# Reordering VectorE's work in a fused attention and two-stage MoE kernel: masks first, gate operations of two tiles alternating, one more buffer

## The chip, the cores and the metric

The kernel runs on one core of one Trainium2 chip. Its time is device microseconds (us) of one execution. Before the change, three runs took 1451.18, 1452.53 and 1453.46 us, so the median is 1452.53 us. A profile of one further execution is what all rows below are read from.

A core has five engines that run their own instruction streams in order and wait for each other through semaphores. TensorE (PE) multiplies matrices, and PEld is its loading of weights. VectorE (DVE) and ScalarE (ACT) work elementwise, as does GpSimd (POOL), and SyncE (SP) issues the DMAs here. The matrix results land in eight PSUM banks; everything else that the engines touch lies in SBUF.

## The reference, cut to what matters

Three steps are chained. A gated linear attention over 4 batches, 8 heads, 768 positions and heads of 48; then a feed-forward layer whose activation is a rational function; then four experts whose outputs are added with weights per token:

```python
f = 1 / (1 + exp(-f_logit))
for t in range(768):
    state = f[t] * state + outer(k[t], v[t]);  y[t] = q[t] @ state
x = y                                        # 3072 tokens x 384
h = x @ w_in                                 # 384 -> 2048
P = a[0] + a[1]*h + a[2]*h**2 + a[3]*h**3
Q = 1 + abs(b[0])*abs(h) + abs(b[1])*h**2
x = (P / (Q + 1e-6)) @ w_out                 # 2048 -> 384
p = probs / (probs.sum(-1) + 1e-9)
out = sum(p[:, e] * (relu(x @ w1[e]) @ w2[e]) for e in range(4))   # 384 -> 1024 -> 384
```

All values are float32. The inputs w_in and w_out of the first layer arrive as 64-bit words, two 32-bit halves each, and are turned into float32 on the chip.

## The kernel before, in words

The 3072 tokens are six chunks of 512 (128 positions of each of 4 batches). The first layer has 16 slots of 128 hidden columns (NJ1), the second has 4 x 8 slots. The first layer's products are called in1 and out1 (lines 836 and 846 as helpers mm_in and mm_out), the second's in2 and out2 (the same two lines). `fused` is one loop over a counter v, with tau = v + 19; manual order: every engine's instructions stand in the order in which this loop emits them. No scheduler moves them.

**The fill.** Chunk 0 has no earlier chunk to overlap with. Its attention runs first, and then for tau from -2 to 17 one slot of the first layer enters per step. Four pieces of work meet on VectorE there:

- Converting weights (`conv`). A slot's conversion has two halves in two consecutive steps. Stage 0 is two mask operations on VectorE (L737 and L738), followed by two operations on ScalarE (L739 and L740). Stage 1 is two more operations on VectorE (L742 and L743) and a product on GpSimd (L746), whose result wf is the slot's weight tile. The table CONV1 says at which step a slot's stage 0 stands; stage 1 stands one step later. `conv_ops(tau)` returns the two lists, and where a step has both, it is the older slot's stage 1 and the newer slot's stage 0.
- The gate, that is the rational function. ScalarE makes h squared, |b h| and a line in h (L894 to L896, `gate_in`). `gate_step` then has a new slot and an old one. For the new slot VectorE makes the denominator (L917) and the numerator (L920 and L921), and ScalarE takes the reciprocal through a logarithm and an exponential (L918 and L919). For the old slot, one step later, VectorE improves the reciprocal (L903 and L904) and multiplies (L911, or L906 in later chunks).
- TensorE's `fill_in` (L874, float32) writes the next slot's h into one of two banks, which become free when L921 has read them. `fill_out` (L881) uses the old slot's gate two steps on.
- At the end, the accumulated sums are split into two parts (L979 and L980) and the second layer starts.

**The mix.** From then on, for each of 192 steps, the second layer's in2 and out2 of the current chunk run, and between them attention and the first layer of the next chunk. For the second layer, ScalarE takes the relu (L934) and VectorE the rest of it (L935, gl), which out2 and the bank's next in2 wait for. Chunks 1 to 5 use the same `gate_step`; there the old slot's result q is copied to a rounded gh on ScalarE (L908) and the rest gl is made on VectorE (L926). `evac2` takes the sum of an expert from three banks: VectorE multiplies into a tile t (L971), GpSimd adds t to the output (L972). The tiles t come from the pool tp, which has two buffers.

Of the kernel before, what the change touches and what calls it, by code (L numbers as in the profile page):

```python
# [8 lines left out]
F32 = mybir.dt.float32  # L9
# [3 lines left out]
AF = mybir.ActivationFunctionType  # L13
ALU = mybir.AluOpType
# [17 lines left out]
QC = 1.0 + 1e-6  # L32
# [299 lines left out]
R = 14  # L332
# [355 lines left out]
def fused(ctx, tc, aps, consts, gm, dp, prep, flag_op):  # L688


    nc = tc.nc
    w1, w2, out = aps["w1"], aps["w2"], aps["out"]
    sc, pn, ident, mask = consts
# [5 lines left out]
    def pool(name, bufs):  # L699
        return ctx.enter_context(tc.tile_pool(name=name, bufs=bufs))  # L700

    wp, x2p, sp, op, pbp, tp, osp = (pool(n, k) for n, k in (
        ("wp", R), ("x2p", 2), ("s1p", 1), ("op", 1), ("pbp", 1), ("tp", 2), ("osp", 2)))
    g1p, g2p, gp = pool("g1p", QC1), pool("g2p", 3), pool("gp", 2)
    att = Att(ctx, tc, aps, consts, gm, banks)

# [44 lines left out]
    def conv_ops(tau):  # L751
        fs = [[], []]
        for i in range(NJ1):
            for k in range(2):
                if tau == CONV1[i] + k * (CONV1[i] >= NB - 6):
                    fs[k].append(partial(conv, i, k))
        return fs
# [39 lines left out]
    def store_all():  # L797
        for k in stores:
            nc.sync.dma_start(out=scr[uses[k]], in_=tile_of[k].bitcast(F32))
        stores.clear()  # L800
# [83 lines left out]
    gate_queue, gate = [], {}  # L884
# [13 lines left out]

    def gate_step(new, old, ops):

        if old:
            q0, r0, y0, _ = gate.pop(old[:2])
            nc.vector.scalar_tensor_tensor(out=q0, in0=q0, scalar=QC, in1=r0, op0=ALU.add, op1=ALU.mult)  # L903
            nc.vector.scalar_tensor_tensor(out=q0, in0=q0, scalar=2.0, in1=r0, op0=ALU.subtract, op1=ALU.mult)  # L904
            if old[0]:
                nc.vector.scalar_tensor_tensor(out=q0, in0=y0, scalar=sc[:, 3:4], in1=q0, op0=ALU.subtract, op1=ALU.mult)  # L906
                gh = g1p.tile([128, 512], F32R, tag="gh", name="gh")
                nc.scalar.copy(out=gh, in_=q0)  # L908
            else:
                gh = g1p.tile([128, 512], F32, tag="gh", name="g")  # L910
                nc.vector.scalar_tensor_tensor(out=gh, in0=y0, scalar=sc[:, 3:4], in1=q0, op0=ALU.subtract, op1=ALU.mult)  # L911
                act1[old[:2]] = gh
        for f in ops[ACT1]:
            f()
        if new:
            q, r, y, h = gate[new[:2]]
            nc.vector.scalar_tensor_tensor(out=q, in0=q, scalar=sc[:, 5:6], in1=r, op0=ALU.mult, op1=ALU.add)  # L917
            nc.scalar.activation(out=r, in_=q, func=AF.Ln, bias=sc[:, 6:7])  # L918
            nc.scalar.activation(out=r, in_=r, func=AF.Exp, scale=-1.0)  # L919
            nc.vector.tensor_tensor(out=y, in0=y, in1=h, op=ALU.mult)  # L920
            nc.vector.scalar_tensor_tensor(out=y, in0=y, scalar=sc[:, 2:3], in1=h, op0=ALU.subtract, op1=ALU.mult)  # L921
        for f in ops[DVE1] + ops[POOL1]:
            f()
        if old and old[0]:
            gl = g1p.tile([128, 512], F32R, tag="gl", name="gl")
            nc.vector.tensor_tensor(out=gl, in0=q0, in1=gh.bitcast(F32), op=ALU.subtract)  # L926
            act1[old[:2]] = (gh, gl)


# [89 lines left out]
    for v in range(-FILL - 6, LAST + 1):  # L1019
        tau = v + FILL  # L1020
        ops = att.begin(v)
        if tau == -5:
            prep()
        if tau + 6 <= NB:
            att.first(tau + 6, conv_ops(tau) if tau + 6 < NB else [[], []])
        store_all()
        items = steps.get(v, [])
        lead = 1 if items and items[0][0] == "in2" and items[0][1] == v + 1 else 0
        fill_run(ops[PA], 9 * lead)
        for item in items[:lead]:  # L1030
            emit(item)
        if 0 <= v < LAST and v not in act2:
            relu(v)
        for f in ops[ACT0]:
            f()
        for u in gate_queue:
            if u[0] and u[:2] not in gate:
                gate[u[:2]] = gate_in(u)
        if 0 <= tau + 1 < NJ1:
            fill_in(tau + 1)  # L1040
        ready = [u for u in gate_queue if u[:2] in gate]
        new = ready[0] if ready else None
        if new:
            gate_queue.remove(new)
        old, pend_old = pend_old, new
        if new or old:
            gate_step(new, old, ops)
        else:
            for f in ops[DVE1] + ops[ACT1] + ops[POOL1]:
                f()  # L1050
        c, k = v // (NE * NJ2) - 1, v % (NE * NJ2)
        if 0 <= c < NCH - 1 and k == 2:
            for b in range(2):
                write_out(c, b + (2 if c else 0), banks[6 + b])
        fill_run(ops[PB], 9 * any(item[0] == "out2" for item in items), True)
        for item in items[lead:]:
            if item[0] == "out2":
                emit(item)
                if run_bounds(v - 1)[1]:
                    evac2(v - 1)  # L1060
        for item in items[lead:]:
            if item[0] == "in2":
                emit(item)
                if v + 1 < LAST:
                    relu(v + 1)
        if 0 <= c < NCH - 1 and k == (1 if c else 2):
            for b in range(2):
                write_out(c, b + (0 if c else 2), banks[6 + b])
        for item in items[lead:]:
            if item[0] == "out1":  # L1070
                emit(item)
        for item in items[lead:]:
            if item[0] == "in1":
                emit(item)
        for u in gate_queue:
            if not u[0] and u[:2] not in gate:
                gate[u[:2]] = gate_in(u)
        if tau == -1:
            spread_probs()
        if 0 <= tau - 2 < NJ1:  # L1080
            fill_out(tau - 2)
        for f in ops[REST]:
            f()
        if v in groups:
            evac1(*groups[v])
        if tau + 6 >= NB:
            for f in sum(reversed(conv_ops(tau)), []):
                f()
        if 10 <= tau and v < -1:
            make_ready(min(R - 6, 2 * (tau - 9)))  # L1090
            split_to(min(AHEAD, state["ready"] - 2))
        if tau == NJ1 + 1:
            for m in range(3):
                split_x2(0, m, acc[m], nc.vector)
            load_pb(0)
        if v >= -1:
            split_to(state["used"] + AHEAD)
        att.loads(v)
        if v == 170:
            flag_op(banks[6], banks[7])  # L1100
# [168 lines left out]
```

## Time and profile before

| what | value |
|---|---|
| median of three runs | 1452.53 us |
| profiled execution, its own time | 1457.07 us |
| its span, first to last instruction | 1455.2 us |
| PE busy | 1375.7 us (95%) |
| DVE busy | 919.0 us (63%) |
| ACT busy | 675.7 us (46%) |
| POOL busy | 289.1 us (20%) |
| mean granted clock of TensorE | 0.978 of full speed |

The span lies 1.9 us below the execution's own time, and this execution is 4.5 us above the median of the three runs. Busy shares are averages over stages that differ: the page's slices of 36.4 us show VectorE at nine tenths and TensorE at eight in the third, fourth and fifth slice, and TensorE at nine tenths or more nearly everywhere from the sixth on. The fill is therefore one stage and the mix another, and they are read apart.

### The profile page before, as it was taken

Reading aid. Unit: us, or ns where it says so; the run is one execution under the profiler, and the core shown is the slowest. Engines: PE = TensorE matmul, PEld = TensorE weight load, DVE = VectorE, ACT = ScalarE, POOL = GpSimd, SP = SyncE. Lnnn points to the kernel's source line nnn. Section 1 sums busy time; section 2 is a strip of 40 time slices with the busy share of each in tenths; the row PEclk is TensorE's granted clock in tenths of the full one; section 3 lists DMA queues with packets and bytes.
Section 4 is the critical chain, followed back from the end, with each engine's and each line's share of the span. In section 5 each row is a group of like instructions: output and inputs, shape, how many; then the busy total and the mean of one; then the engine's idle time right before and its main releaser. Section 6 shows DMA issues by size and latency. Waiting matters only on the chain.

```text
span 1455.2 us, 18263 instructions
## 1 busy us (share of the span) xinstructions
PE 1375.7 (95%) x6502; PEld 1100.6 (76%) x6502; DVE 919.0 (63%) x1403; ACT 675.7 (46%) x1160; POOL 289.1 (20%) x257
## 2 busy tenths in 40 slices
PE   5688899989989999999999999999999999999996
PEld 5533488777768888887888887888888888888885
DVE  7899954879585747575656575566584645562222
ACT  3566644766553554444544543544543544441111
POOL 0122454456442002112002012001012001111010
PEclk8899999999899999999999999999999999999998
DMA  8233685667677556556656656666656766667660
GB/s 302 95 113 124 230 279 207 220 235 255 228 253 235 179 181 212 183 179 229 197 177 214 182 179 214 200 197 211 192 178 214 208 194 195 191 195 239 192 178 25
DMA packets 115699, 287.80 MB, mean 198 GB/s; under 512 B 13104, under 2 KB 31888, under 8 KB 114832
## 3 DMA queue, kind: packets, MB, share of 16 engines
q1 hardware_dynamic: 115024, 286.36, 61.4%
q8 instruction: 54, 0.88, 0.3%
q14 instruction: 45, 0.37, 0.1%
q10 hardware_dynamic: 576, 0.18, 0.0%
HBM read 237.69 MB, written 48.81 MB: 197 GB/s over the span
## 4 chain that ended last, share of the span: by engine, by line
PE 74%; DVE 15%; POOL 3%; issue 3%; DMA 2%; ACT 2%; SPq 0%; POOLq 0%; ACTq 0%; DVEq 0%
PE bank L846 34%; PE bank L836 32%; PE bank L488 2%; DVE t L738 1%; PE bank L464 1%; PE bank L493 1%; POOL w L793 1%; DVE y L920 1%; POOL o L972 1%; DVE t L742 1%; DMA f<-in_qkf_dram 1%; DVE t L743 1%; DVE y L921 1%; PE bank L504 1%; DVE q L904 1%
## 5 line engine op out<-in xcount | busy, mean ns | idle before, releaser
L836 PE MATMUL bank<-x,w 128*128 128x512 f32 x2448 | 609.1, 395 | 9.2 <-DVE gl L935 7.3
L846 PE MATMUL bank<-gh,w 128*128 128x512 f32 x1632 | 530.5, 401 | 6.3 <-DVE t L971 6.3
L836 PEld LDWEIGHTS bank<-x,w 128*128 128x128 f32 x2448 | 453.9, 189 | 104.4 <-DVE gl L935 9.5
L846 PEld LDWEIGHTS bank<-gh,w 128*128 128x128 f32 x1632 | 304.9, 189 | 68.8 <-DVE t L971 7.8
L846 PE MATMUL bank<-gl,w 128*128 128x512 f32 x816 | 325.0, 398 | 0.0
L935 DVE SCALAR_TENSOR_TENSOR gl<-bank,gh 128x512 fp32r<-128x512 f32 x192 | 131.5, 685 | 137.1 <-ACT gh L934 137.1
L972 POOL TENSOR_TENSOR o<-o,t 128x512 f32<-128x512 f32 x69 | 87.5, 1298 | 513.7 <-DVE t L971 513.7
L846 PEld LDWEIGHTS bank<-gl,w 128*128 128x128 f32 x816 | 154.4, 189 | 30.2
L934 ACT ACTIVATE gh<-bank 128x512 fp32r<-128x512 f32 x192 | 113.5, 592 | 124.5 <-PE bank L836 124.5
L917 DVE SCALAR_TENSOR_TENSOR q<-q,sc,r 128x512 f32<-128x512 f32 x80 | 60.2, 752 | 156.6 <-ACT r L895 156.6
L908 ACT CAST gh<-q 128x512 fp32r<-128x512 f32 x80 | 49.4, 618 | 183.2 <-DVE q L906 183.2
L793 POOL TENSOR_TENSOR w<-rawbuf,w 128x384 fp32r<-128x384 f32 x96 | 106.1, 1132 | 98.3 <-ACT w L792 74.8
L890 ACT COPY h<-bank 128x512 f32<-128x512 f32 x80 | 46.9, 586 | 142.6 <-PE bank L836 142.1
L874 PE MATMUL bank<-x,wf 128*128 128x512 f32 x96 | 51.7, 682 | 28.3 <-DVE y L921 21.4
L926 DVE TENSOR_TENSOR gl<-q,gh 128x512 fp32r<-128x512 f32 x80 | 55.1, 689 | 35.0 <-ACT gh L908 35.0
L488 PEld LDWEIGHTS bank<-v,am 128*128 128x128 f32 x384 | 64.9, 201 | 14.4 <-DVE am L475 9.9
L989 DVE TENSOR_TENSOR s<-s,bank 128x512 f32<-128x512 f32 x45 | 30.6, 682 | 71.5 <-PE bank L846 71.5
L971 DVE TENSOR_TENSOR t<-bank,pb 128x512 f32<-128x512 f32 x69 | 46.1, 687 | 45.1 <-PE bank L846 26.7
L488 PE MATMUL bank<-v,am 128*128 128x48 f32 x384 | 60.3, 262 | 9.4 <-DVE am L475 9.4
L904 DVE SCALAR_TENSOR_TENSOR q<-q,r 128x512 f32<-128x512 f32 x80 | 65.5, 819 | 2.8
L906 DVE SCALAR_TENSOR_TENSOR q<-y,sc,q 128x512 f32<-128x512 f32 x80 | 64.8, 810 | 2.8
L903 DVE SCALAR_TENSOR_TENSOR q<-q,r 128x512 f32<-128x512 f32 x80 | 64.4, 805 | 0.0
(102 smaller groups left out, 1413.0 us busy)
## 6 DMA issues: line engine op xcount, KB each, us to landing
w<-ws SPq DMA_DIRECT2D x448, 384.0 KB, 3.6
ws<-w SPq DMA_DIRECT2D x96, 384.0 KB, 4.0
raw<-in_w_dram SPq DMA_DIRECT2D x16, 768.0 KB, 6.8
rawbuf<-in_w_dram SPq DMA_DIRECT2D x64, 192.0 KB, 3.7
f<-in_qkf_dram SPq DMA_DIRECT2D x24, 256.0 KB, 3.7
k<-in_qkf_dram SPq DMA_DIRECT2D x24, 256.0 KB, 4.0
q<-in_qkf_dram SPq DMA_DIRECT2D x24, 256.0 KB, 4.1
w1s<-wf SPq DMA_DIRECT2D x16, 384.0 KB, 3.7
```

What stands on the lines that cost most here:

```text
L488: self.nc.tensor.matmul(self.py[:, o:o + D], self.am[a][:, r], self.v[:, o:o + D], start=(self.c == 0 and r == 0 and a == 0), stop=(r == N ...
L793: nc.gpsimd.tensor_tensor(out=t[:, 1], in0=r, in1=t[:, 0].bitcast(F32), op=ALU.subtract)
L836: nc.tensor.matmul(ps, a[:, o], b[:, kk, :], start=(n == 0), stop=(n == 8))
L846: nc.tensor.matmul(acc[m], a[:, o], b, start=(start and n == 0), stop=(stop and n == last))
L903: nc.vector.scalar_tensor_tensor(out=q0, in0=q0, scalar=QC, in1=r0, op0=ALU.add, op1=ALU.mult)
L904: nc.vector.scalar_tensor_tensor(out=q0, in0=q0, scalar=2.0, in1=r0, op0=ALU.subtract, op1=ALU.mult)
L906: nc.vector.scalar_tensor_tensor(out=q0, in0=y0, scalar=sc[:, 3:4], in1=q0, op0=ALU.subtract, op1=ALU.mult)
L917: nc.vector.scalar_tensor_tensor(out=q, in0=q, scalar=sc[:, 5:6], in1=r, op0=ALU.mult, op1=ALU.add)
L926: nc.vector.tensor_tensor(out=gl, in0=q0, in1=gh.bitcast(F32), op=ALU.subtract)
L934: nc.scalar.activation(out=gh, in_=h, func=AF.Relu)
L935: nc.vector.scalar_tensor_tensor(out=gl, in0=h, scalar=0.0, in1=gh.bitcast(F32), op0=ALU.max, op1=ALU.subtract)
L972: nc.gpsimd.tensor_tensor(out=o[c][:, m], in0=o[c][:, m], in1=t, op=ALU.add)
```

## The change

Three things are changed in `fused`. First, in a step that has both halves of a conversion, the newer slot's stage 0 (the masks) is emitted ahead of the older slot's stage 1. Second, `gate_step` no longer emits the old slot's operations and then the new slot's: in the fill (chunk 0, `late` false) they alternate one by one, and in later chunks (`late` true) the new slot's L917 stands after two of the old slot's three, with ScalarE's logarithm and exponential ahead of the old slot's copy. Third, the pool tp has three buffers. No operation is added or taken away.

```diff
-        ("wp", R), ("x2p", 2), ("s1p", 1), ("op", 1), ("pbp", 1), ("tp", 2), ("osp", 2)))
+        ("wp", R), ("x2p", 2), ("s1p", 1), ("op", 1), ("pbp", 1), ("tp", 3), ("osp", 2)))
...
+        vec = nc.vector
+        late = bool(new and new[0])
         if old:
             q0, r0, y0, _ = gate.pop(old[:2])
-            nc.vector.scalar_tensor_tensor(out=q0, in0=q0, scalar=QC, in1=r0, op0=ALU.add, op1=ALU.mult)
-            nc.vector.scalar_tensor_tensor(out=q0, in0=q0, scalar=2.0, in1=r0, op0=ALU.subtract, op1=ALU.mult)
+            vec.scalar_tensor_tensor(out=q0, in0=q0, scalar=QC, in1=r0, op0=ALU.add, op1=ALU.mult)
+            if late:
+                vec.scalar_tensor_tensor(out=q0, in0=q0, scalar=2.0, in1=r0, op0=ALU.subtract, op1=ALU.mult)
+        if new:
+            q, r, y, h = gate[new[:2]]
+            vec.scalar_tensor_tensor(out=q, in0=q, scalar=sc[:, 5:6], in1=r, op0=ALU.mult, op1=ALU.add)
+            nc.scalar.activation(out=r, in_=q, func=AF.Ln, bias=sc[:, 6:7])
+            nc.scalar.activation(out=r, in_=r, func=AF.Exp, scale=-1.0)
+        if old and not late:
+            vec.scalar_tensor_tensor(out=q0, in0=q0, scalar=2.0, in1=r0, op0=ALU.subtract, op1=ALU.mult)
+        if new and not late:
+            vec.tensor_tensor(out=y, in0=y, in1=h, op=ALU.mult)
+        if old:
             if old[0]:
...
         for f in ops[ACT1]:
             f()
+        if new and late:
+            vec.tensor_tensor(out=y, in0=y, in1=h, op=ALU.mult)
         if new:
-            q, r, y, h = gate[new[:2]]
-            nc.vector.scalar_tensor_tensor(out=q, in0=q, scalar=sc[:, 5:6], in1=r, op0=ALU.mult, op1=ALU.add)
-            nc.scalar.activation(out=r, in_=q, func=AF.Ln, bias=sc[:, 6:7])
-            nc.scalar.activation(out=r, in_=r, func=AF.Exp, scale=-1.0)
-            nc.vector.tensor_tensor(out=y, in0=y, in1=h, op=ALU.mult)
-            nc.vector.scalar_tensor_tensor(out=y, in0=y, scalar=sc[:, 2:3], in1=h, op0=ALU.subtract, op1=ALU.mult)
+            vec.scalar_tensor_tensor(out=y, in0=y, scalar=sc[:, 2:3], in1=h, op0=ALU.subtract, op1=ALU.mult)
...
         if tau + 6 >= NB:
-            for f in sum(reversed(conv_ops(tau)), []):
+            for f in sum(conv_ops(tau), []):
                 f()
```

Lines from 901 on have other numbers afterwards (L903, L904, L911, L917, L920 and L921 become L905, L914, L924, L910, L916 and L931 in the fill). On VectorE, one step of the fill that has both halves of a conversion reads before as follows; bank_97 belongs to the old slot, bank_98 and bank_95 to the new one, L742 and L743 are the older slot's stage 1, and L737 and L738 the newer slot's masks:

```order
L903 SCALAR_TENSOR_TENSOR bank_97<-bank_97,r 128x512
L904 SCALAR_TENSOR_TENSOR bank_97<-bank_97,r 128x512
L911 SCALAR_TENSOR_TENSOR g<-y,sc,bank_97 128x512
L917 SCALAR_TENSOR_TENSOR bank_98<-bank_98,sc,r 128x512
L920 TENSOR_TENSOR y<-y,bank_95 128x512
L921 SCALAR_TENSOR_TENSOR y<-y,sc,bank_95 128x512
L742 SCALAR_TENSOR_TENSOR t<-raw,t 128x768
L743 SCALAR_TENSOR_TENSOR t<-raw,t 128x768
L737 TENSOR_SCALAR t<-raw 128x768
L738 TENSOR_SCALAR t<-raw 128x768
```

The same step on VectorE after the change:

```order
L905 SCALAR_TENSOR_TENSOR bank_97<-bank_97,r 128x512
L910 SCALAR_TENSOR_TENSOR bank_98<-bank_98,sc,r 128x512
L914 SCALAR_TENSOR_TENSOR bank_97<-bank_97,r 128x512
L916 TENSOR_TENSOR y<-y,bank_95 128x512
L924 SCALAR_TENSOR_TENSOR g<-y,sc,bank_97 128x512
L931 SCALAR_TENSOR_TENSOR y<-y,sc,bank_95 128x512
L737 TENSOR_SCALAR t<-raw 128x768
L738 TENSOR_SCALAR t<-raw 128x768
L742 SCALAR_TENSOR_TENSOR t<-raw,t 128x768
L743 SCALAR_TENSOR_TENSOR t<-raw,t 128x768
```

The masks have moved ahead of L742 and L743, and no gate operation directly follows the one whose result it reads. In a mix step with an old and a new slot, VectorE reads before (q and y are tiles of either slot; L935 is the second layer's rest):

```order
L903 SCALAR_TENSOR_TENSOR q<-q,r 128x512
L904 SCALAR_TENSOR_TENSOR q<-q,r 128x512
L906 SCALAR_TENSOR_TENSOR q<-y,sc,q 128x512
L917 SCALAR_TENSOR_TENSOR q<-q,sc,r 128x512
L920 TENSOR_TENSOR y<-y,h 128x512
L921 SCALAR_TENSOR_TENSOR y<-y,sc,h 128x512
L926 TENSOR_TENSOR gl<-q,gh 128x512
L935 SCALAR_TENSOR_TENSOR gl<-bank_96,gh 128x512
```

and after the change, on the same engine at the same place:

```order
L905 SCALAR_TENSOR_TENSOR q<-q,r 128x512
L907 SCALAR_TENSOR_TENSOR q<-q,r 128x512
L910 SCALAR_TENSOR_TENSOR q<-q,sc,r 128x512
L919 SCALAR_TENSOR_TENSOR q<-y,sc,q 128x512
L929 TENSOR_TENSOR y<-y,h 128x512
L931 SCALAR_TENSOR_TENSOR y<-y,sc,h 128x512
L936 TENSOR_TENSOR gl<-q,gh 128x512
L945 SCALAR_TENSOR_TENSOR gl<-bank_96,gh 128x512
```

One pair has changed places: the new slot's denominator (L917, now L910) stands ahead of the old slot's last product (L906, now L919). This happens in 29 steps of the mix, and in the same steps ScalarE's copy gh of the old slot stands behind the new slot's logarithm and exponential instead of ahead of them. The order on TensorE, GpSimd and SyncE is unchanged everywhere.

## Rows read from the trace of the kernel before

**Rows 1.** Busy time by stretch, granted clock (PEclk), DMA share:

```profile
core 0: us, PE busy (x) PEld busy (x) DVE busy (x) ACT busy (x) POOL busy (x), PEclk, DMA share, GB/s
59.20:173.00 113.80, 86.07 (x180) 35.38 (x178) 111.17 (x150) 73.35 (x113) 32.09 (x20) 0.93 0.41 135
...
460.00:1130.00 670.00, 664.95 (x3270) 549.69 (x3269) 427.41 (x663) 318.17 (x540) 83.76 (x75) 1.00 0.63 196
```

**Rows 2.** The second mask operation in that first stretch: busy us, mean ns | idle before:

```profile
L738 DVE TENSOR_SCALAR t<-raw 128x768 int32<-128x768 int32 x11 | 19.0, 1729 | 0.0
```

**Rows 3.** Timeline of one fill step, all engines: start us, us, instruction, idle before:

```profile
87.22 0.55 DVE L738 TENSOR_SCALAR t<-raw 128x768 int32<-128x768 int32 x1
...
87.69 0.69 DVE L903 SCALAR_TENSOR_TENSOR bank<-bank,r 128x512 f32<-128x512 f32 x1
...
88.41 0.70 DVE L904 SCALAR_TENSOR_TENSOR bank<-bank,r 128x512 f32<-128x512 f32 x1
...
89.15 0.75 DVE L911 SCALAR_TENSOR_TENSOR g<-y,sc,bank 128x512 f32<-128x512 f32 x1
...
89.81 0.75 DVE L917 SCALAR_TENSOR_TENSOR bank<-bank,sc,r 128x512 f32<-128x512 f32 x1
...
90.47 0.68 DVE L920 TENSOR_TENSOR y<-y,bank 128x512 f32<-128x512 f32 x1
...
91.19 0.75 DVE L921 SCALAR_TENSOR_TENSOR y<-y,sc,bank 128x512 f32<-128x512 f32 x1
...
91.85 0.95 DVE L742 SCALAR_TENSOR_TENSOR t<-raw,t 128x768 int32<-128x768 int32 x1
91.86 0.58 ACT L894 ACTIVATE bank<-bank 128x512 f32<-128x512 f32 x1
...
92.20 2.74 PE L874 MATMUL bank<-x,wf 128*128 128x512 f32 x6
92.37 0.66 ACT L895 ACTIVATE r<-bank,sc 128x512 f32<-128x512 f32 x1
...
93.59 0.55 DVE L737 TENSOR_SCALAR t<-raw 128x768 int32<-128x768 int32 x1
93.75 2.06 POOL L746 TENSOR_TENSOR wf<-t 128x768 f32<-128x768 f32 x1 [9.19 <-DVE t L743]
...
94.06 2.17 DVE L738 TENSOR_SCALAR t<-raw 128x768 int32<-128x768 int32 x1
...
96.15 0.69 DVE L903 SCALAR_TENSOR_TENSOR bank<-bank,r 128x512 f32<-128x512 f32 x1
```

**Rows 4.** Timeline of a later fill step, with GpSimd beside the gate:

```profile
110.58 0.69 DVE L903 SCALAR_TENSOR_TENSOR bank<-bank,r 128x512 f32<-128x512 f32 x1
110.75 1.81 POOL L746 TENSOR_TENSOR wf<-t 128x768 f32<-128x768 f32 x1 [6.47 <-DVE t L743]
111.31 0.70 DVE L904 SCALAR_TENSOR_TENSOR bank<-bank,r 128x512 f32<-128x512 f32 x1
...
112.12 0.75 DVE L911 SCALAR_TENSOR_TENSOR g<-y,sc,bank 128x512 f32<-128x512 f32 x1
...
114.83 0.55 DVE L737 TENSOR_SCALAR t<-raw 128x768 int32<-128x768 int32 x1
```

**Rows 5.** The chain that ended last, end of the fill: start us, us, what:

```profile
159.42 1.79 POOL wf L746
161.26 4.54 PE bank L874 x6
165.79 7.72 PE bank L881 x18
...
174.61 2.77 PE bank L881 x6
```

**Rows 6.** TensorE's waits, whole span: us in total, times, longest us:

```profile
PE bank L874 <- DVE y L921: 21.4, 9, 5.6
...
PE bank L836 <- DVE gl L935: 7.3, 4, 4.7
PE bank L846 <- DVE t L971: 6.3, 3, 3.7
```

**Rows 7.** VectorE's waits, whole span, the same columns:

```profile
DVE q L917 <- ACT r L895: 156.6, 60, 5.9
...
DVE t L971 <- POOL o L972: 18.4, 22, 1.6
```

More of the change, by code (lines that the diff above doesn't have):

```diff
@@ L899, in gate_step @@
     def gate_step(new, old, ops):
+        vec = nc.vector
+        late = bool(new and new[0])
         if old:
             q0, r0, y0, _ = gate.pop(old[:2])
-            nc.vector.scalar_tensor_tensor(out=q0, in0=q0, scalar=QC, in1=r0, op0=ALU.add, op1=ALU.mult)
-            nc.vector.scalar_tensor_tensor(out=q0, in0=q0, scalar=2.0, in1=r0, op0=ALU.subtract, op1=ALU.mult)
+            vec.scalar_tensor_tensor(out=q0, in0=q0, scalar=QC, in1=r0, op0=ALU.add, op1=ALU.mult)
[11 more added lines that the diff above has]
+        if old:
             if old[0]:
-                nc.vector.scalar_tensor_tensor(out=q0, in0=y0, scalar=sc[:, 3:4], in1=q0, op0=ALU.subtract, op1=ALU.mult)
+                vec.scalar_tensor_tensor(out=q0, in0=y0, scalar=sc[:, 3:4], in1=q0, op0=ALU.subtract, op1=ALU.mult)
                 gh = g1p.tile([128, 512], F32R, tag="gh", name="gh")
@@ L910, in gate_step @@
                 gh = g1p.tile([128, 512], F32, tag="gh", name="g")
-                nc.vector.scalar_tensor_tensor(out=gh, in0=y0, scalar=sc[:, 3:4], in1=q0, op0=ALU.subtract, op1=ALU.mult)
+                vec.scalar_tensor_tensor(out=gh, in0=y0, scalar=sc[:, 3:4], in1=q0, op0=ALU.subtract, op1=ALU.mult)
                 act1[old[:2]] = gh
@@ L925, in gate_step @@
             gl = g1p.tile([128, 512], F32R, tag="gl", name="gl")
-            nc.vector.tensor_tensor(out=gl, in0=q0, in1=gh.bitcast(F32), op=ALU.subtract)
+            vec.tensor_tensor(out=gl, in0=q0, in1=gh.bitcast(F32), op=ALU.subtract)
             act1[old[:2]] = (gh, gl)
```

## The prediction

> **What bounds the kernel now.** I read the busy time by stretch first, because the kernel has a fill and a mix. In the fill, from 59.2 to 173.0 us, VectorE is busy 111.2 of 113.8 us, TensorE 86.1 and ScalarE 73.4 [rows 1]; VectorE is the bound there, and a microsecond taken from it is a microsecond of time until another engine catches up. From 460 to 1130 us TensorE is busy 665.0 of 670 us [rows 1]; what VectorE saves there buys next to nothing. The waits of TensorE say the same: 21.4 us for L921, the last gate operation, which only the fill's L874 waits for, against 7.3 us for gl and 6.3 us for t, the two results of VectorE that the second layer waits for [rows 6]. Then I read the fill step by step in the timeline [rows 3, 4], and at last the chain at its end, which tells where VectorE stops being the bound [rows 5].
>
> **The change part by part: the masks.** In the step of rows 3 the mask L738 takes 2.17 us and hands over to L903 2.09 us after its start (94.06 to 96.15); a step before, it took 0.55 us and handed over after 0.47 us (87.22 to 87.69). The difference stands next to it: GpSimd's L746 runs from 93.75 to 95.81, released by L743, and the long L738 ends 0.42 us after it. So the mask waits until GpSimd is through and then needs its own time. In that stretch the 11 masks take 19.0 us together [rows 2]; with n long ones of 2.17 and 11 - n of 0.55 that is n = 8. These are the eight steps in which an older slot's L743 stands just ahead of a newer slot's masks.
>
> After the change the masks stand ahead of L742 and L743, and L746 starts after both, when the next step's gate operations begin. They last some 3.8 us before the next masks can come, L746 2.06 us, so the two no longer meet. Do the gate operations suffer instead? In rows 4 an L746 stands beside L903, L904 and L911, and these take 0.69, 0.70 and 0.75 us, as without it in rows 3. So each of the eight steps loses 2.09 - 0.47 = 1.62 us, 13.0 us in all. The bounds: 0 if the long time has another cause, 13.0 if none of the eight meets another GpSimd operation.
>
> ScalarE's half of the conversion hangs on the masks too and starts earlier by as much; its user, L742, comes a step later. L746 stands at the end of a step as before.
>
> **The alternation.** In the fill a full step has six gate operations: 0.69 + 0.70 + 0.75 + 0.75 + 0.68 + 0.75 = 4.32 us [rows 3]. Where the next operation does not need the result, it starts 0.09 us before the one ahead of it ends (L911 at 89.15 lasts 0.75, L917 starts at 89.81). Where it does, it starts 0.03 us after the end (L903 to L904, 0.72 us apart). The step lasts 4.16 us now (87.69 to 91.85), and later, with a longer pause ahead of L911, 4.25 us (110.58 to 114.83) [rows 3, 4]. With six neighbours that do not depend on each other it should last 4.32 - 6 x 0.09 = 3.78 us, 0.38 us less early and 0.47 us less later. If the longer pause ahead of L911 stays, it is 0.38 us throughout; I take 0.41. There are 15 full steps, but the last two lie in the tail that TensorE sets (below), so 13 count: 5.3 us, with 4.9 and 6.1 as ends, and 0 as the lower end if a third operation in between does not help.
>
> The Trainium skill speaks against this part. Its page "VectorE: DVE Perf Modes", section "The DRAIN you can't avoid", reports that eight copies on VectorE took the same time with a semaphore after each as with one after the last, and concludes that the pipeline is emptied after each operation anyway and the semaphore costs nothing extra. By that rule the alternation would save nothing. The trace does not agree: the next operation starts 0.09 us before the end without a wait, 0.03 us after it with one. I keep the rule's outcome as a rival.
>
> **The new neighbours.** L917 now stands second in its step instead of fourth, 1.5 us earlier, and needs ScalarE's L895 of the new slot. In rows 3 L895 ended at 93.03, and the step whose L917 needs it began at 96.15, or 94.5 without the long mask; L917 comes 0.6 us into it, so 2 us are left. Only at the end is it close: slots 14 and 15 get their wf one step ahead of use. From the end of L743 that is L746 2.06, L874 2.74, and L894 with L895 up to 1.2 us: 6.0 us, against 3.78 + 1.74 (L742 and L743, 91.85 to 93.59) + 0.6 = 6.1 us on VectorE. If L874 runs as slowly as its last one did (4.54 us, rows 5, after a wait; 2.74 in rows 3), VectorE stalls 1.7 us. I take half, 0.8 us.
>
> **The tail.** From 159.4 us the chain is GpSimd's wf, then TensorE alone: L874 4.54, three slots of L881 7.72, and one more 2.77 us from 174.61 [rows 5]. It starts with L743 of slot 15, so it moves up by what VectorE has gained by then: 13.0 + 5.3 - 0.8 = 17.5 us. Within the tail I count nothing. TensorE cannot overtake earlier: per slot L874 and L881 are 2.74 us each at the faster level, 5.5 us, while VectorE's step has 3.78 us of gate and 0.94, 1.74 or 2.68 us of conversion: 4.7 to 6.5 us, 5.8 on average over a cycle of four slots with three conversions.
>
> **The mix.** In 29 steps L906 and L917 change places and the copy gh follows the exponential. Where VectorE does not wait, it is the same work in the same time, less one dependent pair (0.1 us). Where L917 waits for L895, which it does 60 times in the whole span, 2.6 us on average [rows 7], L906 now stands behind that wait, and what follows on VectorE (both numerator operations, gl of the gate, then L935 of the second layer, L971 and the sums) comes up to 0.66 us later. L935 has room: TensorE waited noticeably for it 4 times in 192, 7.3 us in all [rows 6]. I cost this at 0, with 0.66 us at each of those four places, 2.6 us, as the bad end. The copy gh comes some 1.3 us later on ScalarE, but two numerator operations stand on VectorE before anything reads it, and out1 needs it a step or more afterwards. The third buffer takes away L971's waits for L972: 18.4 us in 22 places on VectorE [rows 7]. But it is the third tile of a set that waits, and TensorE waits for t in 3 places only, 6.3 us [rows 6], for the first tile. I take 0; 3 us, half of that, is the good end.
>
> **The sum.** 1455.2 - 17.5 = 1437.7 us of span, 1439.6 us with the 1.9 us around it. The profiled execution is 4.5 us slower than the median, so I take the difference off the median: 1452.5 - 17.5 = 1435.0 us.
>
> **The rivals.**
> - The alternation saves nothing, by the mechanism above. For it: the long rows differ from the short ones by hundredths only, which the profiler's own stamps might make. Against it: the pattern repeats in each step. Then VectorE gains 13.0 us, without the stall, as it comes later: 1439.5 us.
> - The masks are not freed: they still meet a GpSimd operation, or their wait goes to L742, because GpSimd's other work (splitting weights, which begins in the fill's last steps) comes to stand there. For it: GpSimd is busy 32.1 us in the fill [rows 1], more than 2.06 us for each of 12 slots, 24.7 us, make. Against it: until then GpSimd has only L746 to do. If half of the eight waits stay, 6.5 + 5.3 = 11.8 us are gained, 1440.7; if all do, 5.3, and it is 1447.2 us.
> - The mix gains too: TensorE's waits for gl and t, 13.6 us together [rows 6], lie where VectorE is behind, and 0.1 us a step and freer evacuations take a third, 4.5 us: 1430.5 us.
> - Slower than before: L906 behind L917's wait makes VectorE late for L935 in the mix. The place is the 29 steps, the price 0.66 us each, 19.1 us, and each stop of TensorE makes the following matrix products slow, as the 4.54 us against 2.74 us show, which adds 1.8 us at a few places. It decides once L935's room is below 0.66 us in most of the 29 steps: 1452.5 - 17.5 + 19.1 + 1.8 = 1455.9 us. Against it: four noticeable waits in 192 steps.
>
> **How the numbers follow.** The forecast has 0.66, no gain from the alternation 0.11, masks not freed 0.10, the mix gaining too 0.10, slower 0.03. The forecast's own ends are 17.5 + 0.8 + 0.8 + 3 = 22.1 us (1430.4) and 4.9 + 13.0 - 1.7 - 2.6 = 13.6 us (1438.9). The range takes in the first rival, half of the second and the third: 1429.5 to 1443.5 us. A measurement of this kernel tells about 0.2%, 2.9 us, from no change. Faster than that are all cases but the last and a mixture of several bad ends: 0.94. Within it 0.03, slower 0.03.
>
> **What would show it.** In the new profile no mask L738 of the fill should last over 1 us, where eight did; the full gate step should last 3.8 us instead of 4.2; VectorE should still be busy over nine tenths of a fill that is some 17 us shorter; and from the start of the second layer to the end the time should be the same within 3 us. I am wrong if masks still end just after a GpSimd operation, if ScalarE or TensorE becomes the bound in the fill (VectorE idle there by more than 5 us), or if TensorE's waits for L935 grow beyond the four.

## The result and the profile after

| | before | after |
|---|---|---|
| median, us (4 runs each, same chip) | 1452.99 | 1436.04 |
| range of the runs, us | 1451.18 to 1454.79 | 1434.58 to 1440.86 |
| profiled execution, us (span) | 1457.07 (1455.2) | 1440.86 (1439.0) |

The ratio (of the means) is 0.9889, with a 95% interval from 0.9862 to 0.9916: 16 us less; the medians differ by 16.95 us. The forecast was 1435.0 us, its range 1429.5 to 1443.5 us.

The profiled execution after is 4.8 us above its median, so stretches are compared and not spans. I cut the span at the first mask of the fill (L737 of slot 4) and at the first sum that leaves the fill's banks (L980, after the change L990), and cut the fill once more at slot 14's L746 on GpSimd. Before, busy time by stretch:

```profile
0.00:55.92 55.92, 37.62 (x288) 35.27 (x288) 42.10 (x90) 21.08 (x34) 1.69 (x8) 0.85 0.65 239
...
55.92:150.82 94.90, 72.15 (x151) 29.61 (x151) 92.48 (x120) 62.22 (x93) 21.83 (x13) 0.93 0.34 111
150.82:176.32 25.50, 20.48 (x56) 9.11 (x57) 24.29 (x40) 13.84 (x23) 10.26 (x8) 0.93 0.72 242
...
176.32:1455.20 1278.88, 1245.41 (x6008) 1026.61 (x6006) 760.10 (x1154) 578.56 (x1010) 255.32 (x229) 0.99 0.64 202
```

The same four stretches of the kernel after the change:

```profile
0.00:60.10 60.10, 44.13 (x288) 41.90 (x288) 42.30 (x91) 21.08 (x34) 1.69 (x8) 0.77 0.62 226
...
60.10:138.53 78.43, 69.16 (x151) 28.90 (x151) 77.98 (x122) 62.17 (x95) 20.14 (x13) 0.96 0.40 132
138.53:162.46 23.93, 21.65 (x56) 9.73 (x57) 21.07 (x39) 12.18 (x22) 10.07 (x8) 0.86 0.84 290
...
162.46:1439.00 1276.54, 1243.40 (x6008) 1025.22 (x6006) 763.03 (x1155) 579.01 (x1010) 255.47 (x229) 0.99 0.63 201
```

The gain is the fill: 120.40 us became 102.36, which is 18.04 less, 16.47 of it ahead of slot 14's wf and 1.57 behind. The rest is 2.3 us shorter, and in kernels below whose rest is the same it lies anywhere from 1273.5 to 1278.9 us, so nothing is read from that. The start is the same work and took 4.2 us longer, at a granted clock of 0.77 instead of 0.85. Whether that is the 4.8 us by which this execution stands above its median is not shown: in the kernels below the start takes from 55.76 to 59.48 us, and one whose profiled execution lies 2.6 us under its median (e13) has a start of 58.74 us. In the first part of the fill VectorE is busy 77.98 of 78.43 us: still the bound. In the second part TensorE is busy 21.65 of 23.93 us, and VectorE is idle 2.9 us.

The second cut does not divide VectorE's work alike: slot 15's masks stand behind it before the change and ahead of it after. A cut that does is slot 15's L743, VectorE's last piece of conversion. Before and after it starts at:

```profile
158.26 0.95 DVE L743 SCALAR_TENSOR_TENSOR t<-raw,t 128x768 f32<-128x768 uint32 x1
...
143.00 0.94 DVE L743 SCALAR_TENSOR_TENSOR t<-raw,t 128x768 f32<-128x768 uint32 x1
```

From the start of the fill that is 102.34 us before and 82.90 us after, 19.44 less. What is left to the end of the fill became longer by 1.4 us, 19.46 us instead of 18.06.

The second mask within the fill of the kernel after, which answers to [rows 2]:

```profile
L738 DVE TENSOR_SCALAR t<-raw 128x768 int32<-128x768 int32 x12 | 6.7, 560 | 0.0
```

One full step after, which answers to [rows 3]:

```profile
66.75 0.55 DVE L738 TENSOR_SCALAR t<-raw 128x768 int32<-128x768 int32 x1
...
67.22 0.95 DVE L742 SCALAR_TENSOR_TENSOR t<-raw,t 128x768 int32<-128x768 int32 x1
...
68.09 0.95 DVE L743 SCALAR_TENSOR_TENSOR t<-raw,t 128x768 f32<-128x768 uint32 x1
...
68.96 0.69 DVE L905 SCALAR_TENSOR_TENSOR bank<-bank,r 128x512 f32<-128x512 f32 x1
69.12 1.82 POOL L746 TENSOR_TENSOR wf<-t 128x768 f32<-128x768 f32 x1 [3.41 <-DVE t L743]
...
69.56 0.75 DVE L910 SCALAR_TENSOR_TENSOR bank<-bank,sc,r 128x512 f32<-128x512 f32 x1
70.22 0.69 DVE L914 SCALAR_TENSOR_TENSOR bank<-bank,r 128x512 f32<-128x512 f32 x1
...
72.07 0.74 DVE L931 SCALAR_TENSOR_TENSOR y<-y,sc,bank 128x512 f32<-128x512 f32 x1
...
72.73 0.55 DVE L737 TENSOR_SCALAR t<-raw 128x768 int32<-128x768 int32 x1
```

No mask is long any more. The step runs from 68.96 to 72.73, 3.77 us, where it took 4.16 to 4.25 [rows 3, 4]. GpSimd's L746 stands beside three gate operations of unchanged length, and itself takes 1.82 us instead of 2.06, as no mask runs when it starts.

The chain at the end of the fill, which answers to [rows 5], starts one slot earlier:

```profile
138.53 1.82 POOL wf L746
...
140.40 5.49 PE bank L874 x6
145.88 2.98 PE bank L881 x6
148.86 2.58 PE bank L874 x6
151.44 7.72 PE bank L881 x18
```

Before, the last wait of TensorE for wf was slot 15's, and slot 15's L874 took 4.54 us [rows 5]; slot 14's took 2.84, though TensorE had stood still 3.33 us for its wf as well. Now TensorE stands still 3.85 us for slot 14's wf and then needs 5.49 us for six products that take 2.74 us for slot 15. The granted clock is 0.50 from 140.40 to 145.80 us, the level of 1.2 GHz, and 1.00 from 148.86 to 151.44 us, the level of 2.4. From there on TensorE is the bound. VectorE feels that at one place:

```profile
147.13 0.76 DVE L910 SCALAR_TENSOR_TENSOR bank<-bank,sc,r 128x512 f32<-128x512 f32 x1 [2.58 <-ACT r L895]
```

The waits over the whole span (engine, line, what it waited for: us, times, longest), which answer to [rows 6, 7]:

```profile
DVE q L910 <- ACT r L895: 167.0, 63, 9.3
...
PE bank L874 <- DVE y L931: 7.0, 5, 3.6
...
PE bank L836 <- DVE gl L945: 6.1, 4, 4.8
...
PE bank L846 <- DVE t L981: 6.0, 2, 3.7
```

L874's wait for the gate fell from 21.4 to 7.0 us. In the mix TensorE waits as before, at four places for gl and at two instead of three for t. VectorE's wait for L982, 18.4 us before [rows 7], is no longer among its waits, and nothing came of it. Its wait for L895 grew from 156.6 to 167.0 us, and TensorE's waits for VectorE in the mix did not grow with it.

### The profile page after: what moved, and what is told of

It reads as the page before. It is cut to its first block, busy times and chain, and to the rows that moved or that the text cites. A ratio compares the mean times of both kernels' runs of the same rounds, so it can differ in the third digit from the quotient of the medians.

```text
span 1439.0 us, 18273 instructions
## 1 busy us (share of the span) xinstructions
PE 1378.3 (96%) x6502; PEld 1105.8 (77%) x6502; DVE 904.4 (63%) x1403; ACT 674.4 (47%) x1160; POOL 287.4 (20%) x257
## 4 chain that ended last, share of the span: by engine, by line
PE 75%; DVE 14%; DMA 3%; ACT 2%; issue 2%; POOL 2%; SPq 1%; POOLq 0%; ACTq 0%; DVEq 0%
PE bank L846 34%; PE bank L836 32%; PE bank L488 2%; PE bank L464 1%; DMA f<-in_qkf_dram 1%; POOL w L793 1%; DVE y L931 1%; PE bank L493 1%; DVE g L434 1%; PE bank L881 1%; DVE q L910 1%; DVE q L905 1%; PE bank L504 1%; DVE q L919 1%; PE bank L874 1%
## 5 line engine op out<-in xcount | busy, mean ns | idle before, releaser
L982 POOL TENSOR_TENSOR o<-o,t 128x512 f32<-128x512 f32 x69 | 89.2, 1323 | 512.0 <-DVE t L981 512.0
L910 DVE SCALAR_TENSOR_TENSOR q<-q,sc,r 128x512 f32<-128x512 f32 x80 | 62.7, 784 | 167.0 <-ACT r L895 167.0
L921 ACT CAST gh<-q 128x512 fp32r<-128x512 f32 x80 | 49.1, 614 | 160.9 <-DVE q L919 160.9
L793 POOL TENSOR_TENSOR w<-rawbuf,w 128x384 fp32r<-128x384 f32 x96 | 104.9, 1120 | 95.6 <-ACT w L792 66.7
L911 ACT ACTIVATE r<-q,sc 128x512 f32<-128x512 f32 x80 | 58.0, 725 | 30.9 <-DVE q L910 23.9
L905 DVE SCALAR_TENSOR_TENSOR q<-q,r 128x512 f32<-128x512 f32 x80 | 65.0, 812 | 0.0
L896 ACT ACTIVATE y<-h,sc 128x512 f32<-128x512 f32 x80 | 64.1, 801 | 0.0
L912 ACT ACTIVATE r<-r 128x512 f32<-128x512 f32 x96 | 60.7, 632 | 3.1
L931 DVE SCALAR_TENSOR_TENSOR y<-y,sc,h 128x512 f32<-128x512 f32 x80 | 60.2, 752 | 2.8
```

The costliest lines, as they stand in the source:

```text
L793: nc.gpsimd.tensor_tensor(out=t[:, 1], in0=r, in1=t[:, 0].bitcast(F32), op=ALU.subtract)
L896: nc.scalar.activation(out=y, in_=h, func=AF.Identity, scale=sc[:, 0:1], bias=sc[:, 1:2])
L905: vec.scalar_tensor_tensor(out=q0, in0=q0, scalar=QC, in1=r0, op0=ALU.add, op1=ALU.mult)
L910: vec.scalar_tensor_tensor(out=q, in0=q, scalar=sc[:, 5:6], in1=r, op0=ALU.mult, op1=ALU.add)
L931: vec.scalar_tensor_tensor(out=y, in0=y, scalar=sc[:, 2:3], in1=h, op0=ALU.subtract, op1=ALU.mult)
L982: nc.gpsimd.tensor_tensor(out=o[c][:, m], in0=o[c][:, m], in1=t, op=ALU.add)
```

## The experiments

All ratios are to the kernel before, timed on the same chip in the same job. "The fill" is the stretch between the two cuts above.

### Each part alone

The conversion order alone (e1):

```
-            for f in sum(reversed(conv_ops(tau)), []):
+            for f in sum(conv_ops(tau), []):
```

> Only the masks are emitted ahead of the older slot's L742 and L743; the gate and the pool tp stay as before. The theory (a mask that starts beside GpSimd's L746 waits until GpSimd is through) gives eight waits of 1.62 us less, 13.0 us: 1440.0 us, no L738 in the fill over 1 us, full gate steps still 4.16 to 4.24 us. Rival (the long masks have another cause, or their wait goes to L742): 1452.5 us with L738 still at 2.17 us or with L742 at 1.5 us or more in the same eight steps.

The alternation in the fill alone (e2; `gate_step_blocks` is the old function):

```
+    def gate_step(new, old, ops):
+        if (new or old)[0]:
+            return gate_step_blocks(new, old, ops)
+        ... the changed gate_step
```

> Only the alternation of the gate operations in the fill; masks, mix and tp as before. The theory (an operation that needs the result of the one just ahead starts 0.03 us after its end, any other 0.09 us before it) gives full steps of 3.77 us and 5.3 us in all: 1447.7 us, with the eight masks still long. Rival (the alternation saves nothing, as the rule on the emptied pipeline says): 1453.0 us and full steps of 4.2 us.

The new order in the mix alone (e3; the same with `if not (new or old)[0]`):

> Only the changed place of L917 ahead of L906 in chunks 1 to 5; fill and tp as before. The theory: nothing, 1453 us within 1.5 us. Rival that the mix gains: its part of the 2.3 us by which the stretch after the fill is shorter in the profile after, 1450.7 us. Rival that L906 behind L917's wait makes the second layer late: 1456 us or more, with more than four waits of TensorE for L935.

The third buffer alone (e4; `("tp", 2)` becomes `("tp", 3)`):

> Only the third buffer of the pool tp. The theory: VectorE no longer waits for L972 in L971 (18.4 us before), but the time stays at 1453 us within 1 us, as TensorE waits for the first tile of a set and not for the third. Rival that the mix gains by freer evacuations: 2 to 3 us, 1450.5 us.

| | median, us | ratio, 95% interval | fill, us (before 120.40) | long masks |
|---|---|---|---|---|
| e1, masks first | 1441.28 | 0.9917, 0.9903 to 0.9931 | 107.75 | 0 |
| e2, fill alternates | 1439.68 | 0.9893, 0.9875 to 0.9910 | 104.43 | 2 |
| e3, mix reordered | 1455.88 | 1.0014, 1.0000 to 1.0027 | 120.42 | 8 |
| e4, third buffer | 1452.89 | 0.9989, 0.9976 to 1.0002 | 120.02 | 8 |

A long mask is a second mask of 2.16 to 2.18 us. Each fill is that of one execution.

e1 is as expected: 12.65 us of the fill, against 13.0, with the gate step still at 4.16 us (89.30 to 93.46). e3 and e4 moved nothing that can be told; for e3 a loss of up to 4 us is not excluded, but the sign that its rival named, more than four waits of TensorE for the second layer's rest, is absent: there are four, 6.3 us in all.

e2 is the surprise. It was to give 5.3 us and gave 15.97 in the fill, nearly all that the whole change gives. Its conversion stands as before, L743 and then the masks. In its first two conflicts the mask is long; in the other six it is not. Timeline of VectorE and GpSimd in e2:

```profile
68.02 0.56 DVE L737 TENSOR_SCALAR t<-raw 128x768 int32<-128x768 int32 x1
68.18 2.06 POOL L746 TENSOR_TENSOR wf<-t 128x768 f32<-128x768 f32 x1 [4.39 <-DVE t L743]
68.48 2.17 DVE L738 TENSOR_SCALAR t<-raw 128x768 int32<-128x768 int32 x1
...
76.08 0.55 DVE L737 TENSOR_SCALAR t<-raw 128x768 int32<-128x768 int32 x1
76.24 2.54 POOL L746 TENSOR_TENSOR wf<-t 128x768 f32<-128x768 f32 x1 [6.00 <-DVE t L743]
76.55 0.55 DVE L738 TENSOR_SCALAR t<-raw 128x768 int32<-128x768 int32 x1
```

In both cases L746 starts 0.16 us after L737 and L738 0.30 to 0.31 us after L746. The first time the mask waits, 2.17 us, and L746 takes 2.06; the second time the mask takes 0.55 and L746 2.54, 0.48 us more, about the 0.47 us from one mask to the next. So the conflict is there in both; only who goes first differs. Where GpSimd waits, no cost is seen: TensorE waits 3.6 us for wf in e2's fill and 6.3 us in the fill before. Six short masks are 6 x 1.62 = 9.7 us, and the step of 3.77 us gives the 5.3 us of the forecast: 15.0 of the 15.97. Another 0.6 us is slot 14's L742, which takes 0.95 us in e2 and 1.57 in the kernel before.

### What makes the mask long

All twelve late products on VectorE, so that none runs beside the masks (e5):

```
-            eng = nc.vector if CONV1[i] < NB - 6 else nc.gpsimd
+            eng = nc.vector
```

> The kernel before with one edit: the last twelve products wf = m * p (L746) run on VectorE instead of GpSimd. Theory (the long second mask is the mask waiting for the GpSimd product that runs beside it): no L738 above 1 us, so 8 x 1.62 = 13.0 us go, and twelve products of about 0.98 us each come onto VectorE, 11.8 us: the fill ends 1 us earlier, the time is about 1452 us, 0.999 of before. Rival (the mask is long for a reason of its own place, such as the product L743 ahead of it or the raw words that it reads): the eight long masks stay and the twelve products are added, 1465 us, 1.008 of before.

The masks held back behind the next step's first gate operation (e8):

```
-            for f in sum(reversed(conv_ops(tau)), []):
+            masks, products = conv_ops(tau)
+            for f in products:
                 f()
+            held.extend(masks)      # emitted in gate_step behind its first operation
```

> The kernel before with the two masks of the new slot moved behind the first gate operation of the next step, so that one operation on PSUM stands between L743 and the masks; both masks still come while the GpSimd product of the older slot runs. Theory A (GpSimd takes what the masks need as soon as no mask is running, and holds it to the end of its product): the product starts in the shadow of the gate operation and takes 1.81 us, and now the first mask, L737, waits for its end: about 1.9 us long, and L738 is 0.55; per slot VectorE loses about 1.3 us instead of 1.62, so eight slots give 2 to 4 us: about 1450 us, 0.998 of before. Theory B (a mask that comes while the product runs breaks in, and only a mask that runs as the product starts decides): both masks 0.55 us, the product longer, 13 us less: 1440 us, 0.991. Theory C (the conflict costs the same 1.62 us wherever the pair stands): 1453 us, no change.

e5 measured 1453.1 us, 0.9989 (0.9978 to 1.0001). No mask is long, the products cost what they should, and the two nearly cancel; the fill is 120.86 us, and the rival's 1465 us is out. The edit also puts each product between L743 and the masks, so by itself it does not tell GpSimd from that neighbour; the six masks of e2 that are short right behind L743 do. Within e5's fill:

```profile
L746 DVE TENSOR_TENSOR wf<-t 128x768 f32<-128x768 f32 x12 | 11.5, 958 | 0.4
...
L738 DVE TENSOR_SCALAR t<-raw 128x768 int32<-128x768 int32 x12 | 6.6, 553 | 0.0
```

e8 measured 1450.76 us, 0.9982 (0.9969 to 0.9995), 2.6 us less, with 0.7 to 4.5 us as the interval; its fill is 116.08 us, 4.3 less. That is theory A: six of its first masks take 1.78 us. One slot of it:

```profile
76.63 0.69 DVE L909 SCALAR_TENSOR_TENSOR bank<-bank,r 128x512 f32<-128x512 f32 x1
76.80 1.80 POOL L746 TENSOR_TENSOR wf<-t 128x768 f32<-128x768 f32 x1 [6.13 <-DVE t L743]
77.23 1.78 DVE L737 TENSOR_SCALAR t<-raw 128x768 int32<-128x768 int32 x1
78.94 0.55 DVE L738 TENSOR_SCALAR t<-raw 128x768 int32<-128x768 int32 x1
```

L746 starts in the shadow of the gate operation and runs unhindered, 1.80 us. Now it is the first mask that waits: it ends at 79.01, 0.41 us after L746, as the second one did in [rows 3]. With e5 and e2 this shows the cause: a mask does not run beside GpSimd's product. In e8 the product that has begun is finished first, and the mask waits for all of it. The Trainium skill says this in "SBUF — State Buffer", section "Who interferes with whom": VectorE's two-port modes and GpSimd share one pair of ports, and whoever issues first keeps it for the whole instruction. e8 agrees, if the masks run in such a mode, which no run shows. In e2 the recorded starts do not fit: L746 started 0.31 us ahead of the second mask and still came second.

### Why the alternation frees masks too

In the kernel before, ScalarE is at work as L743 ends in seven of the eight conflicts, on L896 in six of them; in five of the six freed slots of e2 it had ended about a microsecond earlier. e10 ends it sooner, by emitting the new slot's first operation L917, with Ln and Exp, ahead of the old slot's three:

```
+        early = bool(new and not new[0])
+        if early:
+            ... L917, and ScalarE's Ln and Exp, moved up from behind the old slot's operations
```

> The kernel before with one gate operation of the fill moved: the new tile's first operation L917 (with ScalarE's Ln and Exp behind it) comes ahead of the older tile's three instead of behind them; masks stay behind L743, nothing else alternates. It asks why the alternation alone freed six of the eight long masks though their place behind L743 is the same. In the kernel before, ScalarE still works on its next tile (L896) when L743 ends and L737 begins, in seven of the eight slots, and is long done in the six freed slots of the run with the alternation alone. Theory (what ScalarE does as L743 ends shifts L737 and L746 by the few ns that decide whether the mask or the GpSimd product goes first): with Ln and Exp 2 us earlier ScalarE is done there, about six masks become 0.55 us, the step itself changes by less than 0.2 us, 6 x 1.62 = 9.7 us: about 1443 us, 0.993 of before. Rival (it is the alternation of dependent operations, or VectorE's pace, that matters): the eight masks stay long, 1453 us, 0.999 to 1.001 of before.

The idea fell: 1453.14 us, 1.0006 (0.9996 to 1.0016), with eight long masks, though in five of them ScalarE had finished 1.5 to 1.9 us before L737. Timeline of one of them, where ScalarE's next operation is the one on the mask:

```profile
102.30 0.55 DVE L737 TENSOR_SCALAR t<-raw 128x768 int32<-128x768 int32 x1
102.47 2.06 POOL L746 TENSOR_TENSOR wf<-t 128x768 f32<-128x768 f32 x1 [6.40 <-DVE t L743]
102.77 2.17 DVE L738 TENSOR_SCALAR t<-raw 128x768 int32<-128x768 int32 x1
102.89 0.94 ACT L739 ACTIVATE t<-t,sc 128x768 int32<-128x768 int32 x1 [2.45 <-DVE t L737]
```

Two half alternations followed. With o1, o2, o3 for the old slot's operations and n1, n2, n3 for the new one's, a step stands as o1 o2 o3 n1 n2 n3 before and o1 n1 o2 n2 o3 n3 in e2; e12 has o1 o2 n1 n2 o3 n3, e13 has o1 n1 o2 o3 n2 n3.

> The kernel before with the fill's gate operations in a third order: the older tile's first two back to back, as before, and the last four of a step alternating (new first, new product, older third, new third), so that no operation in the second half of a step follows the one whose output it reads; masks stay behind L743. By the rows, the step is 3.89 us instead of 4.16, 13 steps, 3.5 us. Theory A (what decides whether the mask or the GpSimd product goes first is whether VectorE waited on its own result shortly before L742): six masks become short as in the run with the full alternation, 3.5 + 9.7 = 13.2 us: about 1440 us, 0.991 of before. Theory B (one such wait anywhere in the step is enough to keep the mask behind the product): eight long masks, 1449.5 us, 0.9976.

> The kernel before with the mirror of that order: the first three gate operations of a step alternate (older first, new first, older second), and the last two pairs stand back to back, each reading the result ahead of it. By the rows, the step is 4.04 us instead of 4.16, 13 steps, 1.6 us. Theory A (a wait on its own result shortly before L742 decides): eight long masks, 1451.5 us, 0.999 of before. Theory B (one such wait anywhere in the step): the same. Theory C (any change of order that moves the step's length frees them): six short masks, 1.6 + 9.7 = 11.3 us: about 1441.5 us, 0.992.

e12 measured 1447.14 us, 0.9931 (0.9915 to 0.9948), e13 1452.4 us, 0.9977 (0.9962 to 0.9991). Each has seven long masks and one short one, the seventh of the eight in e12 and the first in e13. So theory A is out, and C is out. The masks decide that and not the time: e12's ratio lies nearer to theory A's 0.991 than to B's 0.9976, but the kernel before took 1456.75 us in that job. B is near, but one free mask in each is not what it says. Only the order without any wait on VectorE's own result freed most of them. The freed one of e12 looks as in e2:

```profile
129.43 0.55 DVE L737 TENSOR_SCALAR t<-raw 128x768 int32<-128x768 int32 x1
129.59 2.54 POOL L746 TENSOR_TENSOR wf<-t 128x768 f32<-128x768 f32 x1 [6.13 <-DVE t L743]
129.90 0.55 DVE L738 TENSOR_SCALAR t<-raw 128x768 int32<-128x768 int32 x1
```

What decides who goes first stays open. The starts of the three instructions differ by no more than some 0.01 us between most long and short cases. A forecast cannot rest on what the starts do not show. The new conversion order needs no such forecast, as it keeps the two apart.

e12's fill is 113.62 us, 6.8 less, and its step 3.90 us as expected: 13 x 0.27 and one mask make 5.1. Of the other 1.7 us, 0.95 lie behind slot 15's L743. e13's fill is 115.70 us, 4.7 less.

### The wait for slot 14

Slots 14 and 15 converted one step earlier, on top of the changed kernel (e7):

```
-CONV1 = (-6, -5, -4, -3, -2, -1, 0, 1, 3, 4, 5, 7, 8, 9, 11, 12)
+CONV1 = (-6, -5, -4, -3, -2, -1, 0, 1, 3, 4, 5, 7, 8, 9, 10, 11)
```

> The changed kernel with the last two slots, 14 and 15, converted one step earlier (10 and 11 instead of 11 and 12 in the table CONV1). Theory (the 2.58 us that VectorE waits at L910 of slot 14 come from the conversion of slot 14 starting too late: TensorE waits 3.85 us for its wf and then runs the six products at the lower clock): the wait goes, the fill is about 2.5 us shorter and the time about 1433.5 us, 0.9985 of the changed kernel, 0.987 of before. Rival (the wait only moves to slot 15 or to TensorE's products behind, as the end of the fill is set by the sums of TensorE): same as the changed kernel, 1436 us, within 0.5 us.

The same with the old order in the mix (e9; chunks 1 to 5 use `gate_step_blocks`, as in e2):

> The changed kernel without the alternation in the mix (there the gate operations stand in blocks, as before) and with slots 14 and 15 converted one step earlier. Theory (the alternation in the mix gives nothing or costs a little, the last single-edit run 1.0014 with its interval from 1.0000 to 1.0027; the earlier conversion gives 2.5 us): 1431.5 to 1433.5 us, 0.986 of before, the fastest of all. Rival (the mix's alternation is worth something once the fill is short): slower than the changed kernel with the earlier conversion alone, 1435 to 1437 us.

e7 with attention's loads issued ahead of the product's store in the fill (e11):

```
+        if tau <= 13:
+            att.loads(v)
         if tau + 6 >= NB:
             for f in sum(conv_ops(tau), []):
                 f()
         ...
+        if tau > 13:
             att.loads(v)
```

> The changed kernel with slots 14 and 15 converted one step earlier, and in the fill the loads of attention (L414) issued ahead of the product's store (L747) of their step. In the run with the earlier conversion alone the wait at L910 of slot 14 went, and 2.6 us of waiting came up at L427, for the load of f, which stands on SP behind the store of slot 15's wf. Theory (the wait was handed from wf to that load by SP's queue): the wait at L427 goes, the fill is about 2.5 us shorter, about 1434 us, 0.987 of before. Rival (the load is late for the traffic of the other loads, or TensorE's sums set the end): the same as with the earlier conversion alone, 1436.5 us, 0.989.

| | median, us (4 runs each) | ratio, 95% interval | fill, us (after 102.36) |
|---|---|---|---|
| e7, slots 14, 15 earlier | 1436.74 | 0.9890, 0.9870 to 0.9910 | 102.52 |
| e9, and the mix as before | 1437.29 | 0.9889, 0.9870 to 0.9908 | 100.23 |
| e11, and loads first | 1434.08 | 0.9872, 0.9857 to 0.9886 | 100.75 |

In e7 the wait at slot 14's L910 is gone, and its L874 and slot 15's take 2.81 us each. But the fill is as long as after the change, and the 1433.5 us of the theory did not come. The rival's time did, at another place than it named. A wait of the same size stands elsewhere, in e7's timeline:

```profile
140.75 0.49 SPq L414 DMA_DIRECT2D f<-in_qkf_dram  x1
...
146.92 0.63 ACT L423 ACTIVATE f<-f 112x512 f32<-112x512 f32 x1 [3.27 <-DMA f<-in_qkf_dram]
...
147.58 0.43 DVE L427 TENSOR_SCALAR f<-f 112x512 f32<-112x512 f32 x1 [2.62 <-ACT f L423]
```

Attention's load of f was issued at 140.75, behind the store of slot 15's wf at 139.40, and used at 146.92. That is 83.37 us after the fill's first mask; in e11 it is issued 79.20 us after it, 4.2 us earlier, and the wait at L427 shrinks to 0.26:

```profile
138.08 0.50 SPq L414 DMA_DIRECT2D f<-in_qkf_dram  x1
...
146.07 0.62 ACT L423 ACTIVATE f<-f 112x512 f32<-112x512 f32 x1
...
146.73 1.24 DVE L427 TENSOR_SCALAR f<-f 112x512 f32<-112x512 f32 x1 [0.26 <-ACT f L423]
```

L427 itself takes 1.24 us there instead of 0.43, and ends 0.28 us after an L793 on GpSimd that runs from 145.72 to 147.69 us.

That the place in SP's queue made the difference is not shown: e9 has e7's queue, and its wait at L427 was only 0.6 us, as its load was used 4.13 us after its issue and e7's 6.17 us. e7 and e9 have the same order throughout the fill, and their fills differ by 2.3 us, so among these three kernels no difference of that size can be put down to an edit. In e7 TensorE also waits 3.26 us for a gate behind that place and then needs 4.54 us for six products of L881, which take 2.84 in e9 and e11. e11 has the lowest median of all, 2 us under the changed kernel, but the intervals overlap: it is not shown to be faster. e9 missed its 1431.5 to 1433.5 us and did not beat e7, so the mix's order is not shown to cost anything either.

## Why the prediction was right

The sum was right, 17.5 us against 18.04 in the fill, and the forecast 1435.0 against 1436.04. The signs came too: no mask over 1 us, a step of 3.77 us, VectorE busy 99.05 of 102.36 us of the fill, four waits for the second layer's rest. In part the sum is luck: up to slot 15's L743 VectorE gained 19.44 us, more than the 18.3 of the two gains, and the tail, forecast to stay as long as it was, took 1.4 us back. By its steps:

- **The bound.** VectorE was the bound of the fill: e1 took 12.24 us of its busy time away (116.77 to 104.53 us) and got 12.65 us of time.
- **The masks, 13.0 us.** Shown by e1 in size, and by e5 and e8 in cause. The text spoke of a mask that waits until GpSimd is through; it had not seen that the order can go the other way. Nor did it count slot 14's L742, which meets another product of GpSimd, L793, and takes 1.57 us before and 0.96 after.
- **The alternation, 5.3 us.** The step is 3.77 us, forecast 3.78. On top of e1 the whole change takes another 5.39 us off the fill (107.75 to 102.36). The rival in which the alternation saves nothing is out: independent neighbours do start before the end of the one ahead. But as a part by itself the term was not understood: alone it gives 15.97 us, since it also turns six of the eight conflicts round. The two parts are not additive (12.65 and 15.97 against 18.04 together). The forecast added the two, which holds where the masks are free already, as nothing is left there for the alternation to free. Its rival in which all masks stay long and the alternation gives 5.3 us (1447.2 us) is not what e2 measured, 1439.68 us.
- **The stall, 0.8 us.** The wait came at slot 14, where it was expected, and at its bad end or beyond: 2.58 us against 1.7, because L874 took 5.49 us and not 4.54. At slot 15 there was none. It also lies behind slot 15's L743 (143.00), not ahead of it, so it moves the tail and not the tail's start. What it cost in all stays open: the fill lost 18.04 us, where the two gains alone are 13.0 + 5.3 = 18.3 us, and without the wait the fill was 102.52 us in e7 and 100.23 in e9, against 102.36.
- **The tail, nothing.** Wrong in its place and in size: the chain of TensorE alone begins at slot 14's wf, not slot 15's, and from slot 15's L743 on the fill became 1.4 us longer. The slow L874 has moved from slot 15 (4.54 us, now 2.74) to slot 14 (2.84, now 5.49). Nor does every stop make products slow, as the rival of a slower kernel has it: the 2.84 us came after a stop of 3.33 us.
- **The mix, nothing, and the third buffer, nothing.** Right within what can be told (e3, e4). In e4's waits L972 is gone, TensorE waits 6.0 us for t instead of 6.3, and the time did not move.

## What to carry to other kernels

When one instruction of a kind has two lengths, look at what the other engines run beside it: here the product on GpSimd that ended 0.42 us before each long mask. Then keep the two apart in the order of the work and do not trust which of them comes first, since a change of order elsewhere can turn it round. And when two edits act on the same wait, price each with the other in place: apart, they need not add up to what they give together.

## What the runs showed of the hardware that was not expected

- A mask (tensor_scalar, 128x768 int32) and a product on GpSimd of the same size exclude each other both ways: 2.17 us for the second mask with L746 at 2.06, or 0.55 for it with L746 at 2.54, at starts that differ by about 0.01 us. Gate operations with an operand in PSUM are not touched (0.69 to 0.75 us beside L746).
- The split of weights on GpSimd, L793, does the same to a mask. In e1 slot 15's L737 meets one, takes 1.18 us and ends 0.42 us after it:

```profile
135.33 1.96 POOL L793 TENSOR_TENSOR w<-rawbuf,w 128x384 fp32r<-128x384 f32 x2 [6.25 <-ACT w L792]
...
136.53 1.18 DVE L737 TENSOR_SCALAR t<-raw 128x768 int32<-128x768 int32 x1
```

- An operation with two tiles of SBUF as inputs meets L793 too. In the kernel before, slot 14's L742 runs beside two of them that end at 149.00 us, and takes 1.57 us where the others take 0.95:

```profile
148.24 1.57 DVE t L742
```
